# The last batch of a hand-ordered fused kernel in another order, and its weight-conversion turns placed anew

## The chip, the core and the metric

One core of a Trainium2 chip runs the whole program. TensorE (PE) does the matrix products, VectorE (DVE), ScalarE (ACT) and GpSimd (POOL) the rest, and SyncE (SP) issues the DMAs. The metric is the time of the device in microseconds, the median of three runs.

## What is computed

The reference is an attention without a softmax over the scores, a gated MLP and a token and channel mixer, one after the other, on 8 batches of 576 tokens and 512 channels:

```python
q_s = exp(q - max(q, -1)); q_s = q_s / (sum(q_s, -1) + 1e-09)
k_s = exp(k - max(k, 2));  k_s = k_s / (sum(k_s, 2) + 1e-09)
x = einsum('bhsd,bhde->bhse', q_s, einsum('bhsd,bhse->bhde', k_s, v))
h = gelu_tanh(x @ w_in); u, v = h[..., :512], h[..., 512:]
v_n = (v - mean(v)) / sqrt(var(v) + 1e-06) * g_ln
y = x + (u * (einsum('ts,bsd->btd', w_sg, v_n) + b_sg)) @ w_out
u = y + transpose(transpose(y) @ U @ V)
out = u + maximum(u @ w_ch1, 0) @ w_ch2
```

## The kernel before, in words

Every float32 product is made of three: each operand is split into a high part (a rounded copy, ScalarE, line 61) and a low part (the difference, VectorE or GpSimd, line 55), and TensorE adds high by high, low by high and high by low (`prod`, line 52). The weights `w_ch1` and `w_ch2` come as 64-bit floats and are converted on the chip.

The work of one batch has these stages, named after their PSUM tiles. **xT** makes `px` (x transposed, one tile for each of 4 blocks of channels). **V** makes `pv` for tokens 0 to 4 (`emit_Vh`), then gelu and the layer norm (`stats`, `emit_ln`); between them the previous batch's y is transposed (`pt`, `emit_yT`), multiplied by U (`pp`, `emit_U`, whose result is `pst`) and by V (`pw`, `emit_PV`, added to `yt`). **Uh** makes `pu` in four parts f, **S** the spatial product `pS` in four parts, each followed by `gt` (times g_ln, plus bias), the gate (`gt` times `ut`) and its split into `gh` and `gl`. Then come `pk` and `pt` of the next batch's attention, and **y** makes `py` in four blocks c (`emit_y`, each 24 products), each followed by `yt <- py, x`; between blocks 1 and 2 and between 2 and 3 stand the transposes of the next batch's q (`emit_qT`, copied out by `qh` on ScalarE and `ql` on VectorE). The pool `ps2` of the big PSUM tiles has three buffers, which all these stages take in turn: a tile can be written only when the reader of the third tile before it is done.

After batch 7 come the channel MLP's steps in a seven-product scheme, each step with its combined weight `wu` loaded from DRAM (`wd`): the first 7 (`step`, PSUM tiles `pm`) with the rest of batch 7's y and V between them, then 273 others (`mm`) to the end.

All the while the weights are converted, 176 pieces in a pipeline. A *turn* of it does one of each: a load `stg` (SP), a clamp (POOL, line 171), an exponent step `f <- stg` (ACT, line 177), a merge of the words (DVE, lines 183 and 184) or the sum of two earlier pieces (`f <- f, f`, line 55, POOL or DVE), the copy `chw <- f` of the high part (ACT), the low part (`chw <- f, chw`, POOL or DVE) and the store to `wd` (SP). The table `TURNS[b][stage][slot]` says where in a batch the turns stand (`slot`); `STEP_TURNS` and `GROUP_TURNS` do so for the steps after. Before batch 7's steps 127 turns have been taken.

TensorE and VectorE issue in the order in which the program is written (`in_order(dve)`). For ScalarE, GpSimd and SyncE a scheduler sets the order between batch 0 and the steps after batch 7.

Of the kernel before, what the change touches and what calls it, by code (L numbers as in the profile page):

```python
# [22 lines left out]
def fused_kernel(tc, q, k, v, w_in, g_ln, w_sgT, b_sg, w_out, U, V, w_ch1, w_ch2, outT):  # L23
# [793 lines left out]
    def u_parts(g, kc):  # L817
# [506 lines left out]
    for b in range(B):  # L1324
# [13 lines left out]
        for t in range(NT + 1):  # L1338
            emit_Vh(b, t)
            if nxt:  # L1340
                with behind(dve):
                    for t2 in Q_MAX[b > 0][t]:
                        q_max(nxt, t2)
                    for _ in range(FOLDS[b > 0][t]):
                        next(fold)
            if t < NT:
# [271 lines left out]
```

## Time and profile before

| what | before |
|---|---|
| median of three runs | 1294.39 us (1291.79 to 1294.62) |
| the profiled execution | 1292.16 us, of which its span is 1290.4 us |
| TensorE busy | 1261.8 us, 98% of the span |
| VectorE busy | 969.8 us, 75% |
| ScalarE busy | 653.3 us, 51% |
| GpSimd busy | 324.3 us, 25% |
| mean granted TensorE clock | 0.989 of full speed |

The span runs from the first to the last instruction of the profiled execution; the 1.8 us beside it lie around it. A busy TensorE is not one at its peak, as the ends of its pipelined matmuls are modelled; so the gaps between the starts of its matmuls are what a reader compares. In this kernel matmuls of 512 columns start 0.23 us apart, of 288 columns 0.135 us, and of 128 columns 0.09 us, when nothing holds them up.

### The profile page before, as it was taken

The page shows a single profiled execution, that of the slowest core. Times are in us where ns is not written, and L with a number is a line of the kernel's source. Part 1 is how long each engine was busy: PE and PEld are TensorE (multiplying, and loading weights), DVE is VectorE, ACT ScalarE, POOL GpSimd, SP SyncE. Part 2 cuts the span into 40 slices and gives each one's busy share as a digit, 9 for nine tenths or more (in the row PEclk, how much of TensorE's full clock was granted, in tenths as well). Part 3 has the DMA queues.
Part 4 walks back from the last instruction along what each step waited for, and adds up shares of the span by engine and source line. Part 5 has one row for each costly group of instructions (what it writes and reads, how often), then busy time and mean ns, then how long its engine had stood idle before and what let it go on. Part 6 is the DMA issues. An engine that isn't in the chain of part 4 may idle for free.

```text
span 1290.4 us, 20684 instructions
## 1 busy us (share of the span) xinstructions
PE 1261.8 (98%) x7628; PEld 1142.8 (89%) x7628; DVE 969.8 (75%) x1406; ACT 653.3 (51%) x998; POOL 324.3 (25%) x421
## 2 busy tenths in 40 slices
PE   6999999999999999999999999999999999999998
PEld 5798999999998989797887888888888889999998
DVE  6898889797988888788769943597347953694485
ACT  5756667675757576754563512443224522451342
POOL 4734152623333334663630202000200002000000
PEclk8899999999999999999999999999999999999999
DMA  8515161715343352568998676678766788898786
GB/s 271 167 55 167 51 207 51 235 51 167 99 158 117 113 170 76 195 202 284 397 346 295 213 257 235 220 246 281 259 189 224 256 286 303 274 314 302 256 297 212
DMA packets 135909, 274.17 MB, mean 212 GB/s; under 512 B 15232, under 2 KB 56704, under 8 KB 135808
## 3 DMA queue, kind: packets, MB, share of 16 engines
q1 hardware_dynamic: 135808, 272.84, 64.0%
q8 instruction: 61, 1.00, 0.3%
q14 instruction: 40, 0.33, 0.1%
HBM read 224.56 MB, written 48.23 MB: 211 GB/s over the span
## 4 chain that ended last, share of the span: by engine, by line
PE 82%; DVE 8%; DMA 4%; ACT 3%; issue 1%; POOL 1%; SPq 1%; DVEq 0%; POOLq 0%; ACTq 0%
PE mm L52 51%; PE pS L52 8%; PE py L52 6%; PE pv L52 5%; PE pu L52 5%; PE px L52 1%; PE pk L52 1%; PE pt L553 1%; PE pt L741 1%; PE pp L52 1%; DVE bst L644 1%; DVE sh L654 1%; DMA wu<-wd 1%; DVE yt L55 1%; PE pm L52 1%
## 5 line engine op out<-in xcount | busy, mean ns | idle before, releaser
L52 PE MATMUL mm<-oh,wu 128*128 128x512 f32 (+1 forms) x1120 | 320.5, 367 | 1.2 <-DMA wu<-wd 1.2
L52 PE MATMUL mm<-uh,wu 128*128 128x512 f32 (+1 forms) x1064 | 303.4, 366 | 0.0
L52 PEld LDWEIGHTS mm<-oh,wu 128*128 128x128 f32 x1120 | 207.1, 188 | 27.6 <-ACT oh L61 1.6
L52 PEld LDWEIGHTS mm<-uh,wu 128*128 128x128 f32 x1064 | 196.6, 188 | 24.1 <-issue 0.2
L52 PE MATMUL mm<-ol,wu 128*128 128x512 f32 (+1 forms) x560 | 205.5, 367 | 0.0
L61 ACT ACTIVATE oh<-h 128x1024 fp32r<-128x1024 f32 (+1 forms) x140 | 135.2, 973 | 125.3 <-PE mm L52 104.6
L52 PE MATMUL mm<-ul,wu 128*128 128x512 f32 (+1 forms) x532 | 194.7, 366 | 0.0
L55 DVE TENSOR_TENSOR ol<-h,oh 128x1024 fp32r<-128x1024 f32 (+1 forms) x140 | 156.4, 1121 | 40.1 <-ACT oh L61 37.2
L55 POOL TENSOR_TENSOR ust<-ust 128x1024 f32<-128x1024 f32 (+1 forms) x16 | 36.3, 2278 | 384.5 <-DMA ust<-u2d 323.6
L55 DVE TENSOR_TENSOR h<-mm,u 128x1024 f32<-128x1024 f32 (+1 forms) x57 | 63.3, 1111 | 83.8 <-PE mm L52 83.8
L52 PEld LDWEIGHTS mm<-ol,wu 128*128 128x128 f32 x560 | 105.1, 188 | 13.2
L55 DVE TENSOR_TENSOR u<-mm,u 128x1024 f32<-128x1024 f32 (+1 forms) x53 | 58.9, 1111 | 73.2 <-PE mm L52 68.1
L52 PEld LDWEIGHTS mm<-ul,wu 128*128 128x128 f32 x532 | 99.9, 188 | 12.1
L55 POOL TENSOR_TENSOR chw<-f,chw 128x256 fp32r<-128x256 f32 x98 | 80.7, 836 | 97.6 <-ACT chw L61 87.6
L55 DVE TENSOR_TENSOR h<-h,h 128x1024 f32<-128x1024 f32 (+1 forms) x80 | 88.9, 1111 | 0.1
L1102 ACT ACTIVATE h<-mm 128x1024 f32<-128x1024 f32 (+1 forms) x19 | 17.8, 938 | 128.3 <-PE mm L52 128.3
L1093 ACT ACTIVATE h<-h 128x1024 f32<-128x1024 f32 (+1 forms) x60 | 58.1, 969 | 33.6 <-DVE h L55 33.6
L61 ACT ACTIVATE chw<-f 128x256 fp32r<-128x256 f32 x112 | 42.5, 411 | 63.6 <-DVE f L184 30.7
L61 ACT ACTIVATE u<-mm 128x1024 f32<-128x1024 f32 (+1 forms) x24 | 22.5, 936 | 96.3 <-PE mm L52 80.0
L171 POOL TENSOR_SCALAR stg<-stg 128x256 f32<-128x256 f32 (+1 forms) x88 | 44.3, 508 | 91.3 <-DMA stg<-in_w_ch_dram 50.4
L52 PE MATMUL pu<-xh,wih 128*128 128x288 f32 x256 | 57.9, 308 | 1.9 <-ACT wih L61 0.6
L52 PE MATMUL pu<-xh,wil 128*128 128x288 f32 x256 | 56.3, 301 | 1.8 <-DVE wil L55 1.8
(177 smaller groups left out, 2661.8 us busy)
## 6 DMA issues: line engine op xcount, KB each, us to landing
wu<-wd SPq DMA_DIRECT2D x280, 512.0 KB, 4.4
wd<-chw SPq DMA_DIRECT2D x112, 256.0 KB, 3.5
stg<-in_w_ch_dram SPq DMA_DIRECT2D x64, 256.0 KB, 3.5
u2d<-yt SPq DMA_DIRECT2D x32, 288.0 KB, 2.3
vt<-in_v_dram SPq DMA_DIRECT2D x32, 256.0 KB, 6.9
qt<-in_q_dram SPq DMA_DIRECT2D x7, 1024.0 KB, 8.2
kt<-in_k_dram SPq DMA_DIRECT2D x7, 1024.0 KB, 6.4
res<-u2d SPq DMA_DIRECT2D x12, 512.0 KB, 5.8
```

The lines of the kernel that those rows point to most:

```text
L52: pe.matmul(out, lhsT, rhs, start=first, stop=last, skip_group_check=onto)
L55: return eng.tensor_tensor(out=out, in0=a, in1=b, op=op)
L61: return act.activation(out, src, AF.Copy)
L171: eng.tensor_scalar(out=hi, in0=hi, scalar1=F64_MOST, scalar2=-F64_MOST, op0=ALU.min, op1=ALU.max)
L553: pe.transpose(pt[:, t * P : (t + 1) * P], qt[:, t, c * P : (c + 1) * P], ident)
L644: dve.bn_stats(out=bst[0:n], in_=ge[0:n])
L654: dve.scalar_tensor_tensor(out=shift[0:n], in0=mv[0:n, 0:1], scalar=-1.0, in1=mv[0:n, 1:2], op0=ALU.mult, op1=ALU.mult)
L741: pe.transpose(pt[0:n, c * P : (c + 1) * P], y_t[b][:, c, t * P : t * P + n], ident)
L1093: act.activation(h, h, AF.Relu)
L1102: act.activation(h_out(j, 11, n), bank, AF.Relu)
```

## The change

- `emit_y` of the last batch writes blocks 0 and 1 side by side: products fc 0 to 2 of both, then fc 3 of both.
- The last batch's V loop is written apart: U and V of batch 6 (`emit_U`, `emit_PV`) come ahead of the batch's own `stats`, turns, layer norm and `emit_yT`.
- In batch 7 the gate of part 2 goes from GpSimd to VectorE (`GATES_POOL`); two layer norm pieces of token tile 4 move one part later in Uh; the preparation of the first steps' operands (`u_first`) is spread in other counts, and its second half uses the buffer `vh4` in place of `vl3`.
- ScalarE gets a hand-written order from Uh to the end of y in batch 7.
- The table of turns: 16, 16, 16, 15, 14, 21 and 29 turns in batches 1 to 7 become 18, 18, 18, 18, 16, 21 and 18. Both make 127 up to the steps, and the steps' own tables stay. In the last batch no turn stands in stage S any more. In batches 1 to 6 turns move from single slots into runs of three and four, above all the slots of S and the first two or three of y; the last slot of y, and the slots of xT, get none.
- In steps 4 to 6 the turns come after `pvs` in place of before it.

```diff
-    GATES_POOL = ((), (2,), (2,), (2,), (2,), (2,), (2,), (2,))
+    GATES_POOL = ((), (2,), (2,), (2,), (2,), (2,), (2,), ())
...
     def emit_y(b, c):
         gh, gl2 = g_t[b]
-        py = ps2.tile([P, 2, 512], F32, tag="big", name="py")
-        cs = slice(c * P, (c + 1) * P)
-        for fc in range(NF):
-            prod(py, wo_h[:, fc, cs], wo_l[:, fc, cs], gh[:, fc], gl2[:, fc], fc == 0, fc == NF - 1)
+        cols = (c,) if b < B - 1 or c > 1 else (0, 1)
+        if c == cols[0]:
+            for x in cols:
+                py_t[x] = ps2.tile([P, 2, 512], F32, tag="big", name="py")
+            for fcs in (range(NF - 1), range(NF - 1, NF)):
+                for x in cols:
+                    cs = slice(x * P, (x + 1) * P)
+                    for fc in fcs:
+                        prod(py_t[x], wo_h[:, fc, cs], wo_l[:, fc, cs], gh[:, fc], gl2[:, fc], fc == 0, fc == NF - 1)
+        py = py_t.pop(c)
...
-        (('', '', '', 'T', ''), ('', '', '', 'T'), ('S', 'T', 'TTTT', 'TTT'), ('TTT', 'TT', 'TTT', 'BT'), ('', '', 'T', 'T', '')),
-        (('TTT', 'TT', 'TT', 'T', 'TT'), ('TT', 'T', 'T', 'TTT'), ('TT', 'T', 'TT', ''), ('TTT', 'TT', 'PT', 'T')),
+        (('', '', '', 'T', ''), ('', '', '', 'T'), ('S', 'TT', 'TTTT', 'TTT'), ('TTT', 'TTTT', 'TTT', 'B'), ('', '', '', '', '')),
+        (('TTT', 'TT', 'TT', '', 'TTT'), ('T', 'T', '', ''), ('', '', '', ''), ('TT', 'TT', 'PT', 'T')),
...
+        else:
+            for t in range(NT + 1):
+                emit_Vh(b, t)
+                if t == 2:
+                    for t2 in range(NT + 1):
+                        emit_U(b - 1, t2)
+                for c in ((), (), (), (0, 1), (2, 3))[t]:
+                    emit_PV(b - 1, c)
                 stats(b, t)
+                if t >= NT - 1:
+                    emit_ln(b, t - 1)
+                slot(TURNS[b][0][t])
+                if 0 < t < NT - 1:
+                    emit_ln(b, t - 1)
                 for t2 in ((2,), (3, 4), (), (), ())[t]:
                     emit_yT(b - 1, t2)
...
-                for _ in range((0, 3, 3, 3)[f]):
+                for _ in range((0, 1, 3, 3)[f]):
...
+            acts = in_order(act)
+            acts.__enter__()
...
+                if s < 4:
+                    slot(STEP_TURNS[s])
...
+                if s >= 4:
+                    slot(STEP_TURNS[s])
```

TensorE has the same 7628 matmuls in the same order, but for the interleaved blocks of y in batch 7. Three pieces of the other engines' order follow.

VectorE in stage V of batch 7, from the layer norm statistics of token tile 2 to the first sums of `yt`; `pst` is what `emit_U` leaves, `f` are conversion pieces. Before:

```order
L184 SCALAR_TENSOR_TENSOR f_6656<-stg,f_6656 128x256
L654 SCALAR_TENSOR_TENSOR sh<-mv 128x1
L55 TENSOR_TENSOR pst<-pp,pst 32x512
L644 BN_STATS bst<-ge 128x6
L645 BN_AGGR mv<-bst 128x2
L646 TENSOR_SCALAR mv<-mv 128x1
L183 TENSOR_SCALAR f_6710<-f_6710 128x256
L184 SCALAR_TENSOR_TENSOR f_6710<-stg,f_6710 128x256
L654 SCALAR_TENSOR_TENSOR sh<-mv 128x1
L55 TENSOR_TENSOR yt<-pw,yt 128x576 x2
```

And now:

```order
L55 TENSOR_TENSOR yh_6740<-pt_6735,yh_6740 64x512
L55 TENSOR_TENSOR pst<-pp,pst 32x512
L644 BN_STATS bst<-ge 128x6
L645 BN_AGGR mv<-bst 128x2
L646 TENSOR_SCALAR mv<-mv 128x1
L183 TENSOR_SCALAR f_6707<-f_6707 128x256
L184 SCALAR_TENSOR_TENSOR f_6707<-stg,f_6707 128x256
L183 TENSOR_SCALAR f_6716<-f_6716 128x256
L184 SCALAR_TENSOR_TENSOR f_6716<-stg,f_6716 128x256
L654 SCALAR_TENSOR_TENSOR sh<-mv 128x1
L55 TENSOR_TENSOR yt<-pw,yt 128x576 x2
```

`pst` now stands directly behind the last transposed piece `yh`, ahead of tile 2's statistics, and the two sums `yt <- pw, yt` come ahead of tile 3's statistics and of a third merge.

VectorE in stage y of batch 6, from block 0's sum `yt` to block 1's and the `ql` behind it. Before:

```order
L55 TENSOR_TENSOR yt<-py,x_5624 128x576
L55 TENSOR_TENSOR f_6109<-f_6109,f_6200 128x256
L183 TENSOR_SCALAR f_6339<-f_6339 128x256
L184 SCALAR_TENSOR_TENSOR f_6339<-stg,f_6339 128x256
L55 TENSOR_TENSOR yt<-py,x_5624 128x576
L55 TENSOR_TENSOR ql<-pt,qh 128x576
```

And now:

```order
L55 TENSOR_TENSOR yt<-py,x_5684 128x576
L183 TENSOR_SCALAR f_6399<-f_6399 128x256
L184 SCALAR_TENSOR_TENSOR f_6399<-stg,f_6399 128x256
L183 TENSOR_SCALAR f_6407<-f_6407 128x256
L184 SCALAR_TENSOR_TENSOR f_6407<-stg,f_6407 128x256
L183 TENSOR_SCALAR f_6443<-f_6443 128x256
L184 SCALAR_TENSOR_TENSOR f_6443<-stg,f_6443 128x256
L183 TENSOR_SCALAR f_6452<-f_6452 128x256
L184 SCALAR_TENSOR_TENSOR f_6452<-stg,f_6452 128x256
L55 TENSOR_TENSOR yt<-py,x_5684 128x576
L55 TENSOR_TENSOR ql<-pt,qh 128x576
```

One sum and one merge stood between the two `yt` rows, and now four merges do.

ScalarE at the turn from batch 6 to batch 7, from the first transposed y tile (`yh`) over the last two blocks of x (`xh`, `x`) to the gelu's table. Before:

```order
L61 ACTIVATE yh_6528<-pt_6523 128x512
L61 ACTIVATE xh<-px 128x576 x2
L61 ACTIVATE x_6502<-px 128x576
L61 ACTIVATE yh_6565<-pt_6560 128x512
L61 ACTIVATE x_6502<-px 128x576
L61 ACTIVATE chw<-f_6426 128x256
L61 ACTIVATE chw<-f_6374 128x256
L634 ACT_TABLE_LOAD
```

And now:

```order
L61 ACTIVATE yh_6594<-pt_6589 128x512
L61 ACTIVATE chw<-f_6452 128x256
L61 ACTIVATE chw<-f_6443 128x256
L177 ACTIVATE f_6707<-stg 128x256
L61 ACTIVATE xh<-px 128x576 x2
L61 ACTIVATE x_6568<-px 128x576
L61 ACTIVATE chw<-f_6407 128x256
L61 ACTIVATE yh_6625<-pt_6620 128x512
L177 ACTIVATE f_6716<-stg 128x256
L177 ACTIVATE f_6783<-stg 128x256
L61 ACTIVATE x_6568<-px 128x576
L634 ACT_TABLE_LOAD
```

Three copies `chw` and three exponent steps `f <- stg` have moved in front of the last `x <- px`, where none stood.

## Rows read from the trace of the kernel before

**Rows 1.** The page's part 1: busy us, share of the span, instructions.

```profile
PE 1261.8 (98%) x7628; PEld 1142.8 (89%) x7628; DVE 969.8 (75%) x1406; ACT 653.3 (51%) x998; POOL 324.3 (25%) x421
```

**Rows 2.** Waits of TensorE: us in total, times, longest.

```profile
PE pw L52 <- DVE yt L55: 1.7, 2, 1.3
...
PE mm L52 <- DMA wu<-wd: 1.2, 1, 1.2
...
PE pm L52 <- ACT h L1102: 0.8, 1, 0.8
```

**Rows 3.** Timeline of TensorE, batch 7, stage V: start, us, form, idle before.

```profile
538.39 0.40 PE L52 MATMUL pv<-wih,xl 128*128 128x512 f32 x1
539.05 0.80 PE L52 MATMUL pw<-v_w,pst 128*128 128x288 f32 x4 [0.26 <-DVE pst L55]
...
541.55 0.43 PE L52 MATMUL pw<-v_w,pst 128*128 128x288 f32 x2
543.27 0.53 PE L52 MATMUL pw<-v_w,pst 128*128 128x288 f32 x2 [1.29 <-DVE yt L55]
...
546.96 0.43 PE L52 MATMUL pu<-xh,wil 128*128 128x288 f32 x2
547.85 0.53 PE L52 MATMUL pu<-xh,wih 128*128 128x288 f32 x2 [0.46 <-DVE yt L55]
```

**Rows 4.** Timeline of VectorE, same stretch.

```profile
538.30 0.70 DVE L55 TENSOR_TENSOR pst<-pp,pst 32x512 fp32r<-32x512 f32 x1
...
540.96 1.39 DVE L184 SCALAR_TENSOR_TENSOR f<-stg,f 128x256 uint32<-128x256 uint32 x1
```

**Rows 5.** Timeline of ScalarE, same stretch.

```profile
536.04 0.60 ACT L61 ACTIVATE pst<-pp 128x512 fp32r<-128x512 f32 x1 [0.66 <-PE pp L52]
```

**Rows 6.** Timeline of TensorE, the steps behind batch 7.

```profile
608.46 0.39 PE L52 MATMUL pm<-ul,wu 128*128 128x512 f32 x1
609.24 0.77 PE L52 MATMUL pw<-v_w,pst 128*128 128x288 f32 x2 [0.40 <-DVE yt L55]
```

**Rows 7.** Timeline of VectorE, same steps.

```profile
606.75 0.28 DVE L183 TENSOR_SCALAR f<-f 128x256 uint32<-128x256 uint32 x1
...
608.07 1.48 DVE L55 TENSOR_TENSOR yt<-pw,yt 128x576 f32<-128x576 f32 x3
```

**Rows 8.** Timeline of TensorE, batch 2, stage y.

```profile
231.01 0.51 PE L52 MATMUL py<-gh,wo_h 128*128 128x288 f32 x2
...
241.21 0.71 PE L553 MATMUL pt<-ident,qt 128*128 128x128 f32 x5
```

**Rows 9.** Timeline of VectorE, batch 2, stage y.

```profile
236.82 1.35 DVE L55 TENSOR_TENSOR chw<-f,chw 128x256 fp32r<-128x256 f32 x1
...
239.74 0.42 DVE L184 SCALAR_TENSOR_TENSOR f<-stg,f 128x256 uint32<-128x256 uint32 x1
240.09 0.75 DVE L55 TENSOR_TENSOR yt<-py,x 128x576 f32<-128x576 f32 x1
```

**Rows 10.** Timeline of ScalarE, batch 2, stage y.

```profile
238.21 0.44 ACT L177 ACTIVATE f<-stg 128x256 f32<-128x256 f32 x1 [0.77 <-DVE chw L55]
238.55 0.63 ACT L61 ACTIVATE qh<-pt 128x576 fp32r<-128x576 f32 x1
```

**Rows 11.** Timeline of ScalarE, turn from batch 3 to 4.

```profile
319.30 0.74 ACT L61 ACTIVATE x<-px 128x576 f32<-128x576 f32 x1
```

**Rows 12.** Timeline of TensorE, the same turn.

```profile
321.13 0.48 PE L52 MATMUL pv<-wih,xh 128*128 128x512 f32 x1
```

**Rows 13.** Timeline of ScalarE, turn from batch 2 to 3.

```profile
248.55 0.45 ACT L61 ACTIVATE chw<-f 128x256 fp32r<-128x256 f32 x1
248.86 1.23 ACT L61 ACTIVATE xh<-px 128x576 fp32r<-128x576 f32 x2
```

**Rows 14.** Timeline of VectorE, batch 7, stage S.

```profile
570.42 1.65 DVE L55 TENSOR_TENSOR f<-f,f 128x256 f32<-128x256 f32 x1
```

**Rows 15.** Timeline of GpSimd, batch 7, stage S.

```profile
569.92 1.86 POOL L55 TENSOR_TENSOR gt<-gt,ut 128x576 f32<-128x576 f32 x1 [0.35 <-DVE gt L708]
```

More of the change, by code (lines that the diff above doesn't have):

```diff
@@ L824, in u_parts @@
         else:
-            parts = [wrk.tile([P, F], F32, tag=x, name="us") for x in ("vh2", "vl2", "vh3", "vl3")]
+            parts = [wrk.tile([P, F], F32, tag=x, name="us") for x in ("vh2", "vl2", "vh3", "vh4")]
         parts = [t[:, 0:n] for t in parts]
@@ L1337, in fused_kernel @@
             load_ahead()
[L1338 to L1346, printed above, removed]
-                stats(b, t)
-            slot(TURNS[b][0][t])
-            if t > 0:
-                emit_ln(b, t - 1)
-            if t == NT:
-                stats(b, t)
-            if b > 0:
+        if nxt:
+            for t in range(NT + 1):
+                emit_Vh(b, t)
+                if nxt:
+                    with behind(dve):
+                        for t2 in Q_MAX[b > 0][t]:
+                            q_max(nxt, t2)
+                        for _ in range(FOLDS[b > 0][t]):
+                            next(fold)
+                if t < NT:
+                    stats(b, t)
+                slot(TURNS[b][0][t])
+                if t > 0:
+                    emit_ln(b, t - 1)
+                if t == NT:
+                    stats(b, t)
+                if b > 0:
+                    for t2 in ((2,), (3, 4), (), (), ())[t]:
+                        emit_yT(b - 1, t2)
+                if t == 2 and b > 0:
+                    for t2 in range(NT + 1):
+                        emit_U(b - 1, t2)
+                if b > 0:
+                    for c in ((), (), (), (0, 1), (2, 3))[t]:
+                        emit_PV(b - 1, c)
+        else:
+            for t in range(NT + 1):
+                emit_Vh(b, t)
+                if t == 2:
+                    for t2 in range(NT + 1):
+                        emit_U(b - 1, t2)
+                for c in ((), (), (), (0, 1), (2, 3))[t]:
+                    emit_PV(b - 1, c)
+                stats(b, t)
+                if t >= NT - 1:
+                    emit_ln(b, t - 1)
+                slot(TURNS[b][0][t])
+                if 0 < t < NT - 1:
+                    emit_ln(b, t - 1)
                 for t2 in ((2,), (3, 4), (), (), ())[t]:
                     emit_yT(b - 1, t2)
-            if t == 2 and b > 0:
-                for t2 in range(NT + 1):
-                    emit_U(b - 1, t2)
-            if b > 0:
-                for c in ((), (), (), (0, 1), (2, 3))[t]:
-                    emit_PV(b - 1, c)
         spread_at = 2 if b else 3
@@ L1439, in fused_kernel @@
         for f in range(NF):
+            if not nxt:
+                for _ in range((5, 0, 0, 0)[f]):
+                    next(prep, None)
             emit_S(b, f)
@@ L1447, in fused_kernel @@
                     k_exp(nxt, ((0, 1, 2), (3, 4))[f])
-            if not nxt:
-                for _ in range((2, 0, 0, 0)[f]):
-                    next(prep, None)
             if f > 0:
@@ L1457, in fused_kernel @@
             with tc.issue_after(last['s'].ins):
-                for _ in range(2):
+                for _ in range(1):
                     next(prep, None)
@@ L1526, in fused_kernel @@
                 pvs(s)
-                for _ in range(2 if s == 1 else 0):
+                for _ in range((0, 2, 9, 0, 0, 0, 0)[s]):
                     next(prep, None)
+                if s >= 4:
+                    slot(STEP_TURNS[s])
         gate.clear()
```

18 lines of the change are left out of this document (11 added, 7 removed), and 7 rows, old and new, of the table TURNS.

## The prediction, made before the changed kernel ran

> **What bounds the kernel now.** The page comes first: TensorE is busy for 98% of the span and has nearly as many weight loads beside it [rows 1]. So the kernel is bound by TensorE, its work is the same after the change, and only its gaps can move the time. The second view is TensorE's waits: behind batch 0 they name few things, above all `yt`, one weight load and one `h` [rows 2]. The third is the timeline of TensorE where they fall. Read it by the starts: a gap is the distance of two starts less the usual pitch of what ran between (0.23 us for 512 columns, 0.135 for 288). In batches 1 to 6 I find only the small gaps that recur in each batch (1 us together); from batch 7's stage V on there are some 7 us in a dozen places, and behind the load of `wu` at 685 us none to the end. The change can win a part of those 7 us, and it can lose what it makes TensorE wait for in batches that had no wait.
>
> **What it wins, in batch 7 and the steps behind.** Four gaps are VectorE's order.
>
> 1. `pst`: TensorE goes from 538.39 to 539.05, 0.66 less one pitch of 0.23, a gap of 0.43 us [rows 3]. VectorE starts it at 538.30 [rows 4], though ScalarE had its half by 536.64 [rows 5]: statistics and two merges stood between. Now it stands behind `yh` alone, so it can end by 536.64 + 0.70 = 537.3, ahead of the 538.6 at which TensorE wants it. All 0.43 goes.
> 2. The first two `yt`: 541.55 to 543.27 is 1.72 less two pitches of 0.135, a gap of 1.45 us [rows 3]. In front of them stood tile 3's statistics and a merge that took 1.39 us [rows 4]. Now they follow tile 2's statistics (1.0 us, an estimate from the starts of that group), two merges (1.4) and a shift: from 537.3 the first ends by 540.7, where TensorE wants it at 541.2. All 1.45 goes.
> 3. The other two `yt`: 0.89 less 0.27, a gap of 0.62 us [rows 3], of which the batches before keep 0.22 at that place. 0.40 goes.
> 4. In the steps: 0.78 less 0.23, a gap of 0.55 us [rows 6]. Two merges, from 606.75 to 608.07, stood ahead of the sums [rows 7] and now stand behind them. 0.55 goes.
>
> Together 2.83 us. Three gaps stay. `gl` in stage y holds TensorE for 0.7 us; with the gate of part 2 on VectorE the order is still part 3's bias, its gate, then the `gl` that is late, so interleaving blocks 0 and 1 moves only part 3's `gl`, which was in time. `h` (0.8 of idle) still stands behind the same rows of ScalarE. And `wu` (1.2) is a matter of loads that the change doesn't touch [rows 2]. The gate on VectorE costs some 0.76 us there, in an idle stretch, and frees it of a sum that took 1.65 us [rows 14] beside that gate on GpSimd [rows 15]: nothing on the path. The same goes for `vh4` in place of `vl3`, for the layer norm pieces and for ScalarE's hand order. The eleven turns fewer in batch 7 give room on engines that aren't late there, beyond the merges counted above; should that room be needed, it is worth the gaps listed and no more.
>
> **What it may lose, in batches 1 to 6.** The turns are now in runs, and two places have a deadline.
>
> *Stage y.* The PSUM buffer of block 1 is wanted by the second pair of transposes, in batch 2 at 241.21, which is 10.20 us after `py` begins [rows 8]. Its `yt` must be done by then. In batch 2 four merges and a slow low part already stood before it, and it ended at 240.84, 0.37 us in time [rows 9]. Batch 6 now has four merges there and batch 1 three, and in both, two of ScalarE's exponent steps now stand behind `qh`, which in batch 2 came last [rows 10]. From the end of that `qh` (239.18) I add one step (0.34), two merges of 0.66 each and a `yt` of 0.75: 241.59, 0.38 late; if ScalarE is free as soon as the transposes land, about 0.3 us sooner, it is all but in time. I take 0.3 for each of the two batches, 0.6 together. In batches 3 and 4 one low part waits behind `qh`; batch 2's row [rows 9] had the like and was in time: nothing, at worst 0.45 each. Bounds: nothing below; above, 0.9 in batches 1 and 6 (one low part of 1.35 us [rows 9] in place of a quick one) and 0.45 in the two others, 2.7 us.
>
> *Turn to the next batch.* ScalarE copies out x's blocks back to back there; the last ends at 320.04 [rows 11] and the second `pv` needs its PSUM buffer at 321.13 [rows 12], so there is 1.09 us to spare. One copy `chw` was already between in batch 2's turn, at 0.31 us from start to start [rows 13], and TensorE waited for nothing. Now six stand there from batch 6 to 7: three copies of 0.31 and three steps of 0.34, 1.95 us, 0.86 over. From 3 to 4 there are four, 1.3 us, 0.2 over; the others fit. That is 1.1 us. Bounds: nothing, if ScalarE reaches the stretch earlier than I think; above, 2.0, if the low part of the last block, which stands behind the same copies, is what ends last.
>
> **Sum.** -2.8 + 0.6 + 1.1 = -1.1 us. The profiled execution took 1292.16 us, so its like is 1291.0; the median of the runs is 1294.39, 2.2 us above it, and I forecast against the median: **1293.3 us**. A measurement here tells 0.2%, 2.6 us, from no change. That is about the size of the whole gain.
>
> **The rivals.**
>
> *A, the forecast (0.40):* wins as above, part given back in batches 1 to 6: 1293.3, between 1292 and 1294.5.
>
> *B, the new waits are hidden (0.33):* the order of ScalarE and GpSimd lets the steps through in time, as batch 2 did with four merges. Then 1294.39 - 2.8 = 1291.6; and if `wu` or `h` is in time by luck of the new order, up to 2.4 less, 1289.2. For it: 0.37 us to spare in the fullest stage y. Against it: two exponent steps behind `qh`, six of ScalarE's in front of the last x.
>
> *C, given back at the weight loads (0.12):* TensorE comes to 683 us earlier, but loads and stores fill the DMA queues around that wait, and `wu` lands when it did. Then the gap of 1.2 us [rows 2] grows by the gain before it, and the net is about 0: 1294.4. Against it: the loads are issued as buffers come free, so they should move along.
>
> *D, slower (0.15):* VectorE's merges, now packed in runs beside GpSimd's clamps and low parts, stretch. A merge's second half has taken 0.42 [rows 9] and 1.39 us [rows 4]; a sum took 1.65 with a GpSimd gate running beside it [rows 14, 15]. If two of the merges ahead of block 1's `yt` stretch by 1 us in each of batches 1 and 6, and one in 3 and 4, `yt` passes the 10.20 us by 2.3, 2.3, 1.0 and 1.0: 6.6 + 1.1 - 2.8 = +4.9, and with half the stretches hitting, +1.6. It decides from a `yt` that ends over 10.2 us after `py` begins. I price it at three quarters of it, about +3.2: 1297.6. Against it: batch 2's last three merges ran at full speed. The Trainium skill (GPSIMD Engine Reference, Specifications) says that GpSimd shares its SBUF interfaces with VectorE, with contention where a VectorE instruction has two SBUF inputs; line 184 has two. By that rule the stretch is to be had wherever the two engines meet, so D's price would be the ordinary one; the trace agrees in the sum beside the gate, and doesn't in the three quick merges, beside which GpSimd was mostly idle.
>
> *That the change doesn't do what it says* is excluded for the order of VectorE, which is written by hand; for ScalarE's it is part of B.
>
> **How the numbers follow.** Faster by over 0.2% (under 1291.8) is most of B and the lower tail of A: 0.35. Slower by over 0.2% (over 1297.0) is D's larger half and little else: 0.13. Between lie A, C and the rest: 0.52. The range goes from B with one more gap gone (1289.2) to D at two thirds (1296.8). The runs of before spread over 2.8 us by themselves, which is in it.
>
> **What would show it.** In the new timeline of TensorE: no gap ahead of the first `pw` in batch 7, none over 0.1 beyond the usual between the `pw`, and none ahead of the `pw` of step 4; the gaps at `py <- gl`, `pm` and `wu` still there. New: a wait of `pt` for `yt` of some 0.3 in batches 1 and 6, and of `pv` for ScalarE's `x` of some 0.9 at the start of batch 7. If those don't show, B holds; if `pt` waits for over 1 us in several batches beside merges of 0.8 us and more, D does. I'm wrong altogether if a gap opens in the steps behind 613 us, where I expect none to change.

## The result, and the profile after

The change made the kernel slower: 1312.33 us (median of 4 runs, 1309.9 to 1313.69) against 1294.51 us, a ratio of 1.0138 [1.0115, 1.0161]. That is over the upper end of the range (1296.8), and the other way than the forecast.

| what | before | after |
|---|---|---|
| the profiled execution, its span | 1292.16, 1290.4 us | 1309.9, 1308.1 us |
| start of the first `mm` | 613.03 us | 630.85 us |
| from there to the end of the span | 677.4 us | 677.2 us |

All 17.8 us lie ahead of the first `mm`. The page of the changed kernel (its span, part 1, and the chain of waits by engine):

```profile
span 1308.1 us, 20696 instructions
...
PE 1265.6 (97%) x7628; PEld 1142.3 (87%) x7628; DVE 968.9 (74%) x1408; ACT 653.6 (50%) x998; POOL 317.8 (24%) x419
...
PE 57%; DVE 7%; DMA 5%; ACT 3%; issue 2%; POOL 2%; SPq 0%; DVEq 0%; ACTq 0%; POOLq 0%
```

TensorE does the same 7628 matmuls. Its waits, where before the two for `yt` and `wu` stood first behind batch 0 [rows 2] (us in total, times, longest):

```profile
PE pt L553 <- DVE yt L55: 7.2, 4, 3.8
PE px L52 <- ACT chw L61: 4.5, 2, 3.4
...
PE pv L52 <- DVE xl L55: 1.5, 4, 0.6
...
PE py L52 <- DVE yt L55: 0.8, 1, 0.8
PE pm L52 <- ACT h L1109: 0.8, 1, 0.8
...
PE py L52 <- DVE gl L55: 0.5, 1, 0.5
PE mm L52 <- DMA wu<-wd: 0.4, 1, 0.4
```

`pw` no longer waits for `yt` or `pst`; the waits for `h` and `gl` are as before, and that for `wu` is down from 1.2 to 0.4 us. On top stand two kinds that weren't there: `pt` for `yt`, 7.2 us in four places (batches 1, 3, 4 and 6), and `px` for a copy `chw`, 4.5 us in two (at the end of batches 3 and 5). The second name misleads. `px` reads no `chw`; it takes the PSUM buffer of `py`'s block 2, and so needs that block's `yt`. In batch 3 that `yt` ends at 325.37 and the copy at 325.45, and the wait is put down to the later of the two.

The plainest table is that of the distances between the starts of the first `pu` of each batch. A period k to k+1 holds Uh, S and y of batch k and stage V of batch k+1; the last column runs from batch 7's first `pu` to the first `mm`. The letters stand for the experiments below. A profiled execution stands up to 3.0 us from its kernel's median, and where two kernels have every engine in the same order from batch 1 to batch 6 (the two mixed tables below), one period differs by 2.7 us between them. So a difference of 3 us or less in one period is a hint, and the ratios of the medians decide.

| kernel | 1 to 2 | 2 to 3 | 3 to 4 | 4 to 5 | 5 to 6 | 6 to 7 | 7 to `mm` |
|---|---|---|---|---|---|---|---|
| before | 68.66 | 68.67 | 68.66 | 68.66 | 68.68 | 70.43 | 69.09 |
| after | 76.10 | 68.67 | 75.20 | 71.85 | 71.41 | 70.96 | 67.23 |
| a: old table | 68.66 | 69.08 | 68.68 | 68.66 | 68.80 | 68.04 | 73.95 |
| b: new table alone | 77.06 | 68.67 | 74.68 | 71.52 | 71.90 | 72.63 | 69.40 |
| c: `yt` first | 72.75 | 68.67 | 72.75 | 71.49 | 71.29 | 70.29 | 67.11 |
| d: even | 73.37 | 68.74 | 72.06 | 68.67 | 68.99 | 68.19 | 66.73 |
| e: no last slot | 71.08 | 68.68 | 72.99 | 68.67 | 69.00 | 68.11 | 67.05 |
| f: one turn on | 69.44 | 69.74 | 68.89 | 68.66 | 68.66 | 70.90 | 72.04 |
| g: no clamp | 77.39 | 68.67 | 75.34 | 70.70 | 73.38 | 73.42 | 67.00 |
| h: four `stg` | 76.43 | 68.67 | 75.05 | 73.07 | 71.75 | 71.12 | 67.16 |
| i: three `chw` | 77.19 | 68.66 | 75.51 | 74.16 | 72.49 | 73.67 | 67.01 |
| j: order only | 68.67 | 69.16 | 68.66 | 68.67 | 68.66 | 68.36 | 73.94 |
| k: eleven later | 69.25 | 69.32 | 68.66 | 69.60 | 69.48 | 67.99 | 67.00 |

In the changed kernel batches 1 to 5 lose 19.9 us, batch 2 nothing. Batch 6's stage y loses what batch 7's stage V wins and half a microsecond more, and from batch 7's Uh to the steps 1.9 us are won. The largest loss is batch 1's (TensorE's timeline in its stage y):

```profile
171.53 0.43 PE L52 MATMUL py<-gh,wo_l 128*128 128x288 f32 x2
175.79 0.76 PE L553 MATMUL pt<-ident,qt 128*128 128x128 f32 x5 [3.83 <-DVE yt L55]
176.45 0.71 PE L52 MATMUL py<-gh,wo_h 128*128 128x288 f32 x2
...
179.36 0.68 PE L52 MATMUL py<-gh,wo_h 128*128 128x288 f32 x2
...
180.21 0.43 PE L52 MATMUL py<-gh,wo_l 128*128 128x288 f32 x2
```

The gap ahead of `pt` is 175.79 - 171.53 - 0.27 = 3.99 us, at the very place where I expected 0.3. What VectorE did meanwhile:

```profile
167.29 0.84 DVE L184 SCALAR_TENSOR_TENSOR f<-stg,f 128x256 uint32<-128x256 uint32 x1
171.15 0.29 DVE L183 TENSOR_SCALAR f<-f 128x256 uint32<-128x256 uint32 x1 [3.02 <-ACT f L177]
...
173.86 0.34 DVE L183 TENSOR_SCALAR f<-f 128x256 uint32<-128x256 uint32 x1 [1.76 <-ACT f L177]
...
174.99 0.74 DVE L55 TENSOR_TENSOR yt<-py,x 128x576 f32<-128x576 f32 x1
```

`yt` is ready to go, but stands behind three merges, and two of these wait 3.0 and 1.8 us for ScalarE's exponent step `f`. ScalarE:

```profile
168.81 0.66 ACT L61 ACTIVATE qh<-pt 128x576 fp32r<-128x576 f32 x1 [1.89 <-PE pt L553]
170.00 0.73 ACT L61 ACTIVATE chw<-f 128x256 fp32r<-128x256 f32 x2 [0.53 <-POOL f L55]
170.63 0.42 ACT L177 ACTIVATE f<-stg 128x256 f32<-128x256 f32 x1
172.72 0.42 ACT L61 ACTIVATE chw<-f 128x256 fp32r<-128x256 f32 x1 [1.67 <-POOL f L55]
173.40 0.43 ACT L177 ACTIVATE f<-stg 128x256 f32<-128x256 f32 x1 [0.27 <-POOL chw L55]
```

The first of the two steps stands behind `qh` and a pair of copies `chw` that waits for a sum of GpSimd; the second behind a copy, and then GpSimd. GpSimd and SyncE's queue:

```profile
160.45 0.42 POOL L171 TENSOR_SCALAR stg<-stg 128x256 f32<-128x256 f32 x1 [3.26 <-DMA stg<-in_w_ch_dram]
...
169.24 0.73 POOL L55 TENSOR_TENSOR f<-f,f 128x256 f32<-128x256 f32 x1
171.41 0.42 POOL L171 TENSOR_SCALAR stg<-stg 128x256 f32<-128x256 f32 x1 [1.45 <-DMA stg<-in_w_ch_dram]
171.79 0.89 POOL L55 TENSOR_TENSOR f<-f,f 128x256 f32<-128x256 f32 x1
```

```profile
157.87 2.32 SPq L213 DMA_DIRECT2D stg<-in_w_ch_dram  x4
...
168.16 0.33 SPq L213 DMA_DIRECT2D stg<-in_w_ch_dram  x1
```

Neither step waits for its own word. The 64 loads, clamps, steps and merges of these weights can be paired by their order: the two words went out from 157.87 on, had landed by 161.2, and were clamped by 162.97, some ten microseconds ahead of their steps. What the steps wait for is the order of the queues. GpSimd works without a break from 160.45 to 169.97, and the sum at 169.24 is the last piece of that. Then it stands idle for 1.45 us: the merge that ends at 168.13 frees a `stg` buffer; at 168.16 the load goes out; the clamp begins at 171.41, when it has landed. Behind this clamp stand the next sum and the low parts, and on those wait ScalarE's copy at 172.72 and its step at 173.40, and on the step the merge at 173.86. That is 5.7 us from merge to merge, but it isn't one word's way round: the word loaded at 168.16 has its step at 189.68 and its merge at 234.48. GpSimd's queue holds up work that is wanted now behind a word that is wanted 18 us later. Stage y's first two slots asked for seven turns in 6.5 us, after seven in the last two slots of S.

Batch 3 loses most in the same queue, at another place (VectorE, GpSimd, TensorE):

```profile
324.27 0.43 DVE L55 TENSOR_TENSOR f<-f,f 128x256 f32<-128x256 f32 x1 [4.84 <-POOL chw L55]
324.62 0.75 DVE L55 TENSOR_TENSOR yt<-py,x 128x576 f32<-128x576 f32 x1
```

```profile
321.82 0.41 POOL L171 TENSOR_SCALAR stg<-stg 128x256 f32<-128x256 f32 x1 [2.65 <-DMA stg<-in_w_ch_dram]
323.15 0.41 POOL L171 TENSOR_SCALAR stg<-stg 128x256 f32<-128x256 f32 x1 [0.91 <-DMA stg<-in_w_ch_dram]
323.52 0.72 POOL L55 TENSOR_TENSOR chw<-f,chw 128x256 fp32r<-128x256 f32 x1
```

```profile
325.52 0.50 PE L52 MATMUL px<-qh,kh 128*128 128x288 f32 x2 [3.38 <-ACT chw L61]
```

VectorE's sum, written in place, waits 4.84 us for the low part that reads the old value; that low part is GpSimd's, and stands in its queue behind two clamps, each of which waits for its load (2.65 and 0.91 us). The steps of those two words come at 333.73 and 361.22, 12 and 38 us later. Behind the sum waits block 2's `yt`, and on the PSUM buffer that this `yt` reads waits the next batch's `px`. In batch 5 it is the same pair, a sum that waits 3.17 us for a low part and a `yt` behind it.

### The profile page after: what moved, and what is told of

Read it like the earlier page. It is cut to its first block, busy times and chain, and to the rows that moved or that the text cites. A ratio compares the mean times of both kernels' runs of the same rounds, so it can differ in the third digit from the quotient of the medians.

```text
span 1308.1 us, 20696 instructions
## 1 busy us (share of the span) xinstructions
PE 1265.6 (97%) x7628; PEld 1142.3 (87%) x7628; DVE 968.9 (74%) x1408; ACT 653.6 (50%) x998; POOL 317.8 (24%) x419
## 4 chain that ended last, share of the span: by engine, by line
PE 57%; DVE 7%; DMA 5%; ACT 3%; issue 2%; POOL 2%; SPq 0%; DVEq 0%; ACTq 0%; POOLq 0%
PE mm L52 45%; PE pv L52 3%; PE pS L52 2%; DMA wd<-chw 2%; PE py L52 2%; PE pu L52 2%; DMA wu<-wd 1%; DMA stg<-in_w_ch_dram 1%; POOL chw L55 1%; PE pm L52 1%; DVE h L55 1%; DVE yt L55 1%; DVE qt L55 1%; PE pp L52 1%; PE px L52 1%
## 5 line engine op out<-in xcount | busy, mean ns | idle before, releaser
L52 PEld LDWEIGHTS mm<-oh,wu 128*128 128x128 f32 x1120 | 206.9, 188 | 26.4 <-issue 0.2
L55 POOL TENSOR_TENSOR chw<-f,chw 128x256 fp32r<-128x256 f32 x95 | 76.7, 818 | 99.2 <-ACT chw L61 99.0
L1109 ACT ACTIVATE h<-mm 128x1024 f32<-128x1024 f32 (+1 forms) x19 | 17.8, 937 | 127.1 <-PE mm L52 127.1
L52 PE MATMUL py<-gh,wo_h 128*128 128x288 f32 x256 | 58.2, 310 | 3.1 <-DVE gt L708 1.6
```

The lines of the kernel that those rows point to most:

```text
L52: pe.matmul(out, lhsT, rhs, start=first, stop=last, skip_group_check=onto)
L55: return eng.tensor_tensor(out=out, in0=a, in1=b, op=op)
L1109: act.activation(h_out(j, 11, n), bank, AF.Relu)
```

## The experiments

**The table, or the order of batch 7?** Run a takes the table of before in the changed kernel, run b the new table in the kernel before; in both the rest stays. Of run a's rows, batch 1's:

```diff
-        (('T', '', '', '', ''), ('', '', '', ''), ('T', 'T', 'TTTT', 'TTT'), ('TTT', 'TTTT', 'TW', ''), ('', '', '', '', '')),
+        (('T', '', '', '', ''), ('', '', '', ''), ('T', 'T', 'TTT', 'TT'), ('TT', 'TTTT', 'TTW', ''), ('', '', '', '', '')),
...
```

> The changed kernel with the whole table of turns of before, batches 1 to 7; the last batch's new order stays. Theory 1 (the loss is all in the table, the new order of batch 7 gains what its gaps measured): the waits for yt, ql and px in batches 1 to 6 are gone, and the time is 2 to 4 us under before, about 1291.5. Rival (the new loop or ScalarE's hand order of the last batch costs too, hidden behind the table's loss): 1294 or more.

> The kernel before with the new table of turns alone. Theory 1: all the loss and none of the gain, about 1314 to 1316 us, with the waits of pt for yt in batches 1, 3, 4 and 6 as in the changed kernel. Rival (the loss needs the new loop as well): under 1305.

Run a: 1.0019 [1.0003, 1.0034], a little slower than before and not 2 to 4 us faster. Run b: 1.0158 [1.0135, 1.0182]. The table is the loss, as theory 1 has it: in run a batches 1 to 6 lose at most 0.4 us each, in b they lose as in the changed kernel. Stage V of batch 7 wins its 2.4 us in run a (68.04 against 70.43). But then 4.9 us are lost from batch 7's Uh to the steps, in `py` (TensorE, then VectorE):

```profile
574.36 0.54 PE L52 MATMUL py<-gl,wo_h 128*128 128x288 f32 x2 [1.54 <-DVE gl L55]
...
578.12 0.85 PE L52 MATMUL py<-gl,wo_h 128*128 128x288 f32 x2 [2.69 <-DVE gl L55]
```

```profile
574.93 0.94 DVE L55 TENSOR_TENSOR f<-f,f 128x256 f32<-128x256 f32 x1 [0.62 <-POOL chw L55]
```

The 29 turns of the old row leave sums and merges in stage S that VectorE meets with their inputs late (this sum waited 0.62 us for a low part and took 0.94), ahead of the `gt` and `gl` that `py` wants. The new row has no turn there. So with the old row the new order of stage V put off work, and didn't remove it. Run b has the new row without the new order, and wins nothing there either (69.40).

**Where VectorE has `yt`, or how fast the turns can go?** Run c writes the turns of y's slots 1 to 3 behind the block's own `yt` in batches 1 to 6. Run d spreads the turns of batches 1, 3, 4, 5 and 6 evenly over S and y, as many in each batch. Run c's edit, and batch 1's row in run d:

```diff
+            late = nxt and b and c > 0
-            if b or c:
+            if (b or c) and not late:
...
             emit_y(b, c)
-            if b == 0 and c == 0:
+            if late or b == 0 and c == 0:
                 slot(TURNS[b][3][c])
```

```diff
-        (('T', '', '', '', ''), ('', '', '', ''), ('T', 'T', 'TTTT', 'TTT'), ('TTT', 'TTTT', 'TW', ''), ('', '', '', '', '')),
+        (('T', '', '', '', ''), ('', '', '', ''), ('TT', 'TT', 'TTT', 'TT'), ('TT', 'TT', 'TTW', 'TT'), ('', '', '', '', '')),
...
```

> The changed kernel; in batches 1 to 6 the turns of the y slots 1, 2 and 3 are written behind the block's own yt in place of in front of it. Same turns in the same stage, so VectorE does yt of block 1 with only slot 0's merges before it. Theory order (yt stands behind merges, and that is all): the 7.2 us of pt waiting for yt and what follows from them go, 1298 to 1302 us. Theory rate (a run of 14 to 17 turns is faster than the conversion's chain of load, clamp, exponent, merge, sums, copy and low can go, whatever stands behind it): the waits move on to ql, qh and the px of the next batch, and 1307 or more stays.

> The changed kernel with the turns of batches 1, 3, 4, 5 and 6 spread evenly over the slots of S and y, the same number in each batch (18, 18, 18, 16, 21). Theory rate: no slot asks for more than the chain gives, and most of the loss goes, 1293 to 1300 us. Theory count (109 turns by the end of batch 6 in place of 98 are too many for GpSimd, VectorE and the DMA queue beside the rest): over 1306 us, with waits in other places.

Run c: 1.0080 [1.0050, 1.0111], between the two forecasts. The waits of `pt` for `yt` are gone, yet 13.6 of the 19.9 us that batches 1 to 5 lost remain, since the waits have moved on, in batch 1 to `ql` and then to `x`:

```profile
174.52 0.53 PE L52 MATMUL py<-gh,wo_h 128*128 128x288 f32 x2 [2.08 <-DVE ql L55]
...
186.78 0.50 PE L52 MATMUL pv<-wih,xh 128*128 128x512 f32 x1 [1.20 <-ACT x L61]
```

So `yt`'s place is a way by which lateness reached TensorE, worth a third of it, and not its source. Run d: 1.0025 [1.0013, 1.0037]. Batches 4 and 5 lose 0.0 and 0.3 us in place of 3.2 and 2.7 with the same turns and the same start in the cycle: the run was too dense, and the number of turns isn't the reason there. Batches 1 and 3 still lose 4.7 and 3.4. Both have two turns in the last slot of y (as batches 5 and 6 have, which lose at most 0.3), and in batch 1 the wait is at the other end of the conversion, the store (ScalarE, then SyncE's queue, batch 1 to 2):

```profile
195.99 0.42 ACT L61 ACTIVATE chw<-f 128x256 fp32r<-128x256 f32 x1 [3.73 <-DMA wd<-chw]
```

```profile
184.79 3.61 SPq L147 DMA_DIRECT2D vt<-in_v_dram  x4
188.50 9.06 SPq L384 DMA_DIRECT2D wd<-chw  x4
```

The copy waits 3.73 us for a store to give its `chw` buffer back; the stores stand in SyncE's queue behind the next batch's `vt`. ScalarE's gelu and `pst`, and with them TensorE, wait behind the copy.

**The last slot, or the place in the cycle?** Run e is d without turns in that slot in batches 1 and 3 (in the changed kernel itself batch 5 alone has one there); run f is the kernel before with one turn moved from batch 7's first slot to batch 1's first slot of S, so that the rows of batches 2 to 6 are the same and every slot from there to batch 7's first does the next piece of the cycle of 4 word blocks and 7 factors. Run f's edit:

```diff
-        (('T', '', '', '', ''), ('', '', '', ''), ('T', 'T', 'TTT', 'TT'), ('TT', 'TTTT', 'TTW', ''), ('', '', '', '', '')),
+        (('T', '', '', '', ''), ('', '', '', ''), ('TT', 'T', 'TTT', 'TT'), ('TT', 'TTTT', 'TTW', ''), ('', '', '', '', '')),
...
-        (('TTT', 'TT', 'TT', 'T', 'TT'), ('TT', 'T', 'T', 'TTT'), ('TT', 'T', 'TT', ''), ('TTT', 'TT', 'PT', 'T')),
+        (('TT', 'TT', 'TT', 'T', 'TT'), ('TT', 'T', 'T', 'TTT'), ('TT', 'T', 'TT', ''), ('TTT', 'TT', 'PT', 'T')),
```

> The even table once more, with no turn in the last slot of y in batches 1 and 3 (one or two go to the end of Uh, one to y's slots 0 and 2); the numbers of turns, 18, 18, 18, 18, 16, 21 and 18, stay. In the even table batches 1 and 3 alone lost, 4.7 and 3.4 us, where ScalarE's copy chw waited for a store that stood behind the next batch's k and v in SyncE's queue. If turns in the last slot are the reason, those go and the time is 2 to 5 us under before (ratio 0.996 to 0.9985). Rival (it is the pieces' place in the cycle of 11, not the slot): batches 1 or 3 lose again, ratio 1.001 or more.

> The kernel before with a single turn moved from the start of batch 7 (its first slot) to the first slot of S in batch 1 (17 and 28 turns), where nothing stood tight. The rows of batches 2 to 6 are the same, but each slot does the next piece of the cycle of 4 word blocks and 7 factors. Theory rate alone (what counts is how many turns a slot has): batches 2 to 6 keep their 68.66 us, and the time is within 1 us of before. Theory place in the cycle (a slot's cost hangs on which pieces fall in it): batches 2 to 6 together lose 3 us or more.

Run e: 1.0031 [1.0018, 1.0045]. No gain, so its rival. Batch 1 loses 2.4 in place of 4.7, and batch 3 loses 4.3, above all at `yt` (2.0 of idle) and `ql` (0.7): the last slot was at most a part of it in batch 1, and not in batch 3. Run f: 1.0020 [1.0010, 1.0031], and both forecasts miss. The rows 2 to 5, as before word for word, lose 1.3 us together, batch 1 0.8, and stage y of batch 6, which shares its period with stage V, has a new wait for `yt` of 1.0 us. The largest part, 2.9 us, is lost from batch 7's Uh on, where `pu` waits 1.8 us for `yt` and every slot but the first does the piece that it did before. That is the profiled execution, which is 2.5 us above the median. So one turn moved costs 2 or 3 us, but it isn't what costs 20, and run f doesn't show that the place in the cycle is why.

Two more tables put together from rows that had cost nothing (batches 1 and 3 as before, 2 as changed, 4 to 6 even) speak more plainly. In one batch 7 had 22 turns, in the other 18 with four more in the steps.

> The changed kernel with the table put together from rows that cost no wait so far: batches 1 and 3 as before (16 and 16 turns), 2 as changed (18), 4, 5 and 6 spread evenly (18, 16, 21), and batch 7 with 22 turns: the changed row and four turns more in Uh, none in S. By the parts measured: nothing lost in batches 1 to 6, 2.4 us won in stage V of batch 7, about 2 won from its Uh to the steps: 4 to 5 us under before, ratio 0.996 to 0.997. Rival (four turns more in Uh hold up gl in stage y, as the 29 turns did): no gain, ratio 0.999 or more.

> As the one before, but batch 7 with the changed row of 18 turns and the four left over in steps 0 to 3, one each. Same gain if four turns there cost nothing: ratio 0.996 to 0.997. Rival (the steps' merges come late for yt or h): a new wait of pm or pw, ratio 0.998 or more.

They took 1.0056 [1.0043, 1.0069] and 1.0062 [1.0049, 1.0076]. The gain forecast for both didn't come, and not for the rivals' reasons alone. Batch 2's row, free in the changed kernel and at most 1.4 us over in any other run with it, lost 3.8 and 4.9 us there (periods 72.42 and 73.53), where it starts two pieces earlier in the cycle. Batch 4's even row, free in run d, lost 1.8 and 4.5. A row isn't good or bad by itself; its neighbours changed too, so that the place in the cycle is the reason is likely and not shown.

Run e with the turns of y's slot 1 behind the `yt` of block 1 was to show what that wait alone was worth:

> As the one before, and in batches 1 to 6 the turns of y's slot 1 are written behind the yt of block 1. If what is left of waits is that yt, it is faster than the one before by what pt waited there; if the turns then come late for block 2's yt or ql, slower. Theory order: 0 to 1 us faster. Theory rate: 0 to 2 us slower.

1.0049 [1.0032, 1.0065], so about 2 us slower than run e by the medians, as theory rate had it, though the two intervals overlap: batches 3 and 5 lose 1.7 and 2.1 us more.

**Which part of the conversion is it?** Four runs of the changed kernel take away or shorten one. One leaves out GpSimd's clamp of the channel weights' words after batch 0; two have a buffer fewer (`stg`, `chw`); one has seven `f32` buffers for five and four `stg` for five. In all four the scheduler also set ScalarE's, GpSimd's and SyncE's order anew (ScalarE's differs in a dozen places or more in batches 1 to 6, VectorE's in none), so none of them changes one thing alone.

```diff
+        def bound(self):
+            if not gate and nb[0] > 0:
+                return
+            clamped(self.w, self.clamp)
...
-        return stgp.tile([P, S], F32, tag="stg", name="stg", bufs=5)
+        return stgp.tile([P, S], F32, tag="stg", name="stg", bufs=4)
...
-    chw = [((stgp, 4),), 0]
+    chw = [((stgp, 3),), 0]
...
-        t = stgp.tile([P, HS], F32, tag="f32", name="f32", bufs=5)[:, 0:n]
+        t = stgp.tile([P, HS], F32, tag="f32", name="f32", bufs=7)[:, 0:n]
```

> The changed kernel without GpSimd's clamp (line 171) of the channel weights' words after batch 0; everything else, the table too, is the same. It leaves out the clamp of words to a largest value. Theory queue (GpSimd executes in order, and a clamp that waits for its load holds up the low parts and sums behind it, and 0.42 us of work each): the waits of VectorE's sums for chw and of pt for yt fall by half or more, 1298 to 1304 us. Theory chain (what limits a run is the load's landing and the number of f32 and stg buffers, whoever does the clamp): the waits stay at the place where the exponent step now waits for the load itself, 1307 or more.

> The changed kernel with seven f32 buffers in place of five and four stg buffers in place of five (SBUF holds no more). Theory f32 (an exponent step waits for the low part that read its f32 buffer last, so the next four words can't start before the last factors are through): the loss falls to under 8 us, 1294 to 1302. Theory load (what a run waits for is a stg buffer, then 3.3 us of its load): with one buffer fewer it grows, 1312 to 1320.

> The changed kernel with four stg buffers in place of five and nothing else. If a run of turns waits for a free stg buffer and then for its load, batches 1 to 6 lose 3 us or more beyond the changed kernel's (periods against periods). If a run isn't bound there: under 1 us in batches 1 to 6, the rest in batch 0.

> The changed kernel with three chw buffers in place of four. If ScalarE's copy chw waits for the landing of the store three copies back, the longest waits of the changed kernel grow: batches 1 to 6 lose 4 us or more beyond the changed kernel's. If the stores' end isn't where a run is bound: under 1 us.

The times here are of one execution each. Without the clamp (g) it took 1315.59 us, and each forecast is half right: `pt` waits less for `yt` (2.9 us in all in place of 7.2, in batch 1 a gap of 1.05 us in place of 3.99), and the wait of 3.38 us ahead of batch 3's `px` is gone, but now `pv` waits 2 to 3 us for ScalarE's `xh`, and ScalarE waits for stores. Compare that wait in g, in the changed kernel and with three `chw` buffers (i):

```profile
ACT chw L61 <- DMA wd<-chw: 14.5, 8, 4.0
```

```profile
ACT chw L61 <- DMA wd<-chw: 3.2, 5, 1.3
```

```profile
ACT chw L61 <- DMA wd<-chw: 17.3, 15, 3.4
```

With the clamp's work and its waits gone the periods 1 to 7 are 4.7 us longer than the changed kernel's. So the clamps ahead of other work in GpSimd's queue were a link to TensorE; with them away, waits for the stores stood in their place. With one `stg` fewer (h, 1322.22 us) the periods grow by 1.9 us, between the two forecasts, and the rest lies in batch 0, which uses that buffer. There ScalarE's steps wait 16.0 us for clamped words in batches 1 to 6, where in the changed kernel none does: with five buffers its steps weren't held by their own loads. With one `chw` fewer (i, 1323.14 us) the periods grow by 7.5, as forecast for a run that is near its bound at the stores. There `px`'s two waits go by their right name:

```profile
PE px L52 <- DVE yt L55: 4.4, 2, 3.3
```

With two `f32` more and one `stg` fewer (1322.04 us) they grow by 4.6. The steps' waits for a low part to give an `f32` buffer back (9.9 us in the changed kernel, VectorE's and GpSimd's low parts together) are gone, `pt` waits 3.8 us for `yt` in place of 7.2, and the steps wait 26.4 us for clamped words; what more `f32` with all five `stg` would do isn't shown. Taking a `chw` away costs most of those tried, but that the stores bind the changed kernel isn't shown either: ScalarE waits for them 3.2 us there. Larger rings of `stg` or `chw` were not tried.

**Is the gain of batch 7's order to be had without the table?** Run j is the kernel before with the new order of stage V and the turns of steps 4 to 6 behind `pvs`, and nothing else. Run k is the changed kernel with the rows of before in batches 1 to 6, its own row of 18 in batch 7, and the eleven turns left over, one whole cycle, in the first eleven `mm` steps, so that every row keeps its place in the cycle; its twin has them in steps 5 to 16. Run k's steps:

```diff
-    GROUP_TURNS = (2, 2, 2, 2, 2, 2, 2, 2, 2, 2, 3, 3, 2, 3, 4, 1, 2, 1, 3, 3)
+    GROUP_TURNS = (3, 3, 3, 3, 3, 3, 3, 3, 3, 3, 4, 3, 2, 3, 4, 1, 2, 1, 3, 3)
```

> The kernel before with two pieces of the change alone: the new order of batch 7's stage V (U and V of batch 6 ahead of statistics, turns and layer norm) and the turns of steps 4 to 6 behind pvs. Table, gates, y's products, ScalarE's order and the preparation counts are those of before. If the loss of the old table under the new code (gl late in stage y of batch 7) came from the other pieces, this has the gain alone: V 2.3 us, the steps 0.5 to 1, ratio 0.9965 to 0.9985, faster than both kernels. Rival (29 turns in batch 7 and the new V order alone make gl late): 1.000 or more, with a wait of py for gl over 1 us.

> The changed kernel with the rows of batches 1 to 6 as before (98 turns), the changed row of batch 7 (18), and the eleven turns left over, one whole cycle, in the first eleven mm steps, one more in each. So every row stands at the place in the cycle for which it was used, batches 1 to 6 as in the kernel before and batch 7 as in the changed one. By the parts measured: nothing lost in batches 1 to 6 (68.66 us each), 2 to 2.4 us won in stage V of batch 7 and 2 from there to the first mm: ratio 0.996 to 0.998, faster than both kernels. Rival (the later weights land late for wu, or ScalarE and VectorE are late in those steps): a wait of mm of 1 us or more behind 613 us, ratio 0.999 or more.

> As the one before, with the eleven turns in mm steps 5 to 16 in place of 1 to 11. If the room there is the same, the same ratio within 0.001; if the first steps are where ScalarE and VectorE are tight, it is the better of the two; if the weights come late, it is the worse one, with a wait of mm for wu.

Run j: 1.0014 [1.0002, 1.0026], the rival. It wins 2.1 us in stage V and loses 4.9 behind, with waits of `py` for `gl` and `gh`:

```profile
572.23 0.53 PE L52 MATMUL py<-gl,wo_h 128*128 128x288 f32 x2 [0.82 <-DVE gl L55]
...
573.82 0.53 PE L52 MATMUL py<-gl,wo_h 128*128 128x288 f32 x2 [0.53 <-DVE gl L55]
...
577.42 0.85 PE L52 MATMUL py<-gh,wo_h 128*128 128x288 f32 x2 [2.80 <-ACT gh L61]
```

Run k: 1.0044 [1.0031, 1.0056], the rival; its twin 1.0048 [1.0034, 1.0061], the same within 0.001. The gain appears in full, 2.4 us in stage V and 2.1 behind, and batches 1 to 6 are within a microsecond of before each. Then the steps with three turns lose twice as much, in waits of `mm` that the kernel before doesn't have:

```profile
629.18 0.73 PE L52 MATMUL mm<-uh,wu 128*128 128x512 f32 x2 [1.10 <-DVE h L55]
...
643.79 0.70 PE L52 MATMUL mm<-uh,wu 128*128 128x512 f32 x2 [1.53 <-DMA wu<-wd]
...
655.55 0.93 PE L52 MATMUL mm<-uh,wu 128*128 128x512 f32 x2 [2.10 <-DVE h L55]
```

No version tried beats the kernel before.

## Why the prediction was wrong

**The gain was right in place, and under-sized.** All four gaps are gone, gap 3 too, of which I had left 0.22 us standing. Stage V of batch 7 in the changed kernel shows `pw` with no idle ahead of it:

```profile
560.71 0.69 PE L52 MATMUL pw<-v_w,pst 128*128 128x288 f32 x4
...
563.09 0.69 PE L52 MATMUL pw<-v_w,pst 128*128 128x288 f32 x4
```

In the runs with quiet batches (a, d, e, k) stage V is 2.2 to 2.4 us shorter, where items 1 and 2 said 1.88, and what follows is 1.9 to 2.4 us shorter wherever batch 7 has the new order and 18 turns and the steps only their own, where items 3 and 4 said 0.95. The short restarts behind a removed wait go with it (0.40 behind the second `yt`, 0.33 in the steps), and I had left them standing. `gl` and `h` stayed at 0.5 and 0.8 us of idle, as said. `wu` I had called untouched: its wait at 685 us is gone, and one of 0.4 stands elsewhere.

**The step that failed is the pricing of stage y.** "From the end of that `qh` (239.18) I add one step (0.34), two merges of 0.66 each and a `yt` of 0.75": this lets every merge start as soon as the engine in front of it is free. Put to batch 1, where `qh` ends at 169.47, it says 171.88; `yt` ended at 175.73, 3.85 us later. The place and the deadline were right, in batches 1 and 6, and batches 3 and 4, which I had put at nothing, wait there too (1.10 and 1.58 us of idle). What failed is that a step follows `qh`, or the step before it, at once. The first step began 1.16 us behind `qh`, since two copies stood between that waited 0.53 us for GpSimd's sum; the second began 2.35 us behind the first, since its copy and its `f32` buffer waited for GpSimd, and GpSimd 1.45 us for the load of a later word; the last merge took 0.5 us more than I gave it. So VectorE waited 3.0 and 1.8 us ahead of two merges, and TensorE's gap was 3.99 us in place of 0.3, beyond the upper bound of 0.9. The bound came from batch 2 [rows 9, 10], which has eleven turns in the last two slots of S and the first two of y; batch 1 now has fourteen. I followed what is queued on VectorE and a part of what is queued on ScalarE, and neither GpSimd's queue nor the loads and buffers that it waits for. My reason for B, that batch 2 had gone through with four merges, was the wrong measure, as it leaves out the turns in the slots before. A count of those is no full measure either: batch 5 has seven turns in the same four slots and loses 2.7 us.

**The turn to the next batch** was 1.1 us in the sum, for ScalarE's copies of `x`. At 6 to 7, where I had put 0.86, it is 0.5 us. At 3 to 4 it is 3.5 and at 5 to 6 1.3 us, but ahead of `px` and for another reason, block 2's `yt`, late behind a sum. This second deadline of stage y I had not counted at all.

**"Room on engines that aren't late there"**, of the eleven turns fewer in batch 7, was wrong too: the gain needs them. With 29 turns the new order loses 4.9 us behind stage V (runs a and j), and what it wins is 2.4; and the 18 turns without the new order win nothing (run b).

**The rivals.** D had the sign and the point from which it decides, a `yt` that ends over 10.2 us after `py` begins. The sign that I gave for it, waits of over 1 us in several batches beside merges of 0.8 us and more, came true in batches 1, 3 and 4, and yet its mechanism isn't the main one. Ahead of batch 1's `yt` two merges' second halves took 0.62 and 0.83 us for 0.42, which makes 0.6 us of the 4.0; GpSimd's clamps and low parts from 160.84 to 164.2 were slow too, by 1.5 us, of which ScalarE, busy with `qh` until 169.47, shows at most 0.5. For most of the rest VectorE is idle for want of inputs. Of the rule of the Trainium skill cited for it (GPSIMD Engine Reference, Specifications) the trace shows that much: line 184 took 0.84 us at 167.29 with GpSimd busy beside it, and 0.43 at 176.63 with GpSimd idle. C, a gain given back at `wu`, didn't happen in the changed kernel. Two thirds of D's stretch would have been +2.7 by its own figures, 1297.1 and not 1296.8; nothing hangs on it.

Shown are that the table is the loss (runs a and b), that the density of its runs costs batches 4 and 5 theirs (run d), and, by the trace, that the two largest waits reach TensorE through GpSimd's queue. Which buffer or engine would bind a dense run next isn't settled by g, h and i. Why batch 1 loses 4.0 at `pt` and batch 2 nothing, with 18 turns each, is told only in part: batch 2 has twelve turns in those four slots, and its place in the cycle differs. How the two shares divide isn't settled.

## What to carry to other kernels

Work that runs in the background of a bound engine passes through queues that are done in order. Before such work is packed more densely, follow each wanted result back through every one of them, to a DMA or a buffer: a piece that nobody needs yet, and that waits for its load, can hold up one that is needed now. When a gap is closed by putting such work off, look for the place where it comes due; here it cost more there, in three different places, than the gap. And a row of a hand-tuned table that costs nothing at one place and beside one neighbour can cost 4 us at another: measure it again when it moves.

## What the runs showed of the hardware

A long wait costs more than itself. Windows of the changed kernel (us, busy time and instructions of PE, PEld, DVE, ACT and POOL, granted clock, DMA share, GB/s): the wait in batch 1, the stretch behind it, and the stretch behind a wait of 1.10 us in batch 3.

```profile
171.50:175.70 4.20, 0.46 (x4) 0.21 (x2) 2.40 (x5) 1.72 (x4) 3.77 (x6) 1.00 0.50 185
175.80:179.40 3.60, 3.60 (x18) 3.46 (x19) 2.56 (x5) 1.26 (x3) 0.85 (x2) 0.62 0.65 178
...
318.00:321.00 3.00, 2.97 (x22) 2.83 (x23) 1.40 (x3) 1.36 (x3) 0.43 (x1) 1.00 1.04 301
```

Behind 3.83 us without a matmul the granted clock was 0.62 of full speed on the mean for the next 3.6 us, and the matmuls of 288 columns started 0.24 us apart in place of 0.135: the 1.2 GHz level, until they were at 0.135 again from 180 us on, the 2.4 GHz level. That cost seven pairs times 0.21, 1.5 us on top of 4.0. Behind the wait of 3.38 us in batch 3 it was 0.65 for the next 4.5 us. Behind the waits of 1.10 and 1.58 us the clock stayed at 1.00. The Trainium skill (TensorE: Matmul & The Clock Gate, Why this matters for your kernels) warns that idle gaps between bursts of matmuls bring the array back to its slower clock; the trace agrees for the two long waits and shows none of it for the short ones. In the forecast this term was missing, because no wait in it was that long.
